# Gate projection of two token groups by seven block products, and output sums formed in PSUM banks

## The chip, the cores and the metric

The kernel runs on one core of a Trainium2 chip. Its time is the device time of one execution in microseconds (us). Five engines work side by side, each through its own list of instructions: TensorE (PE in the profile; PEld is its loading of weights), VectorE (DVE), ScalarE (ACT), GpSimd (POOL) and SyncE (SP). They wait for one another by semaphores. TensorE writes its products into PSUM, [...]; VectorE and ScalarE read them there.

## The reference

Attention with cosine-weighted features is followed by a gated feed-forward block.

```python
# q, k, v: (8, 8, 576, 64);  w_gate, w_val: (512, 1536);  w_out: (1536, 512)
q_p, k_p = phi(q, cos_w, sin_w), phi(k, cos_w, sin_w)      # relu, times cos and sin
kv = np.einsum('bhsf,bhsd->bhfd', k_p, v)
z = np.sum(k_p, axis=2)
num = np.einsum('bhsf,bhfd->bhsd', q_p, kv)
den = np.einsum('bhsf,bhf->bhs', q_p, z)[..., None] + 1e-06
attn_out = num / den
x = attn_out.transpose(0, 2, 1, 3).reshape(4608, 512)
g = x @ w_gate
silu = g * (1.0 / (1.0 + np.exp(-g)))
val = x @ w_val
return silu * val @ w_out                                  # (4608, 512), float32
```

## The kernel before

The 4608 tokens are worked through in nine groups (`tg` 0 to 8) of 512. A group has a projection part of 12 blocks `fc` of 128 features, and then an output stage. Beside them, in numbered slots, runs the attention work of later groups: `phi_q` (the `r_q` products), `vmul` and `kv_mm` per batch, and four attention tiles per group, whose result `x` is turned by DMA into `xT`, the input of the next group.

A block of the projections is eight matmuls of 512 columns, a silu on ScalarE and a multiplication on VectorE:

```python
def ffn_mm(tg, fc, ...):                    # cut to the case of a whole group
    st["f", ...] = [take(1)[:, 0:n] for _ in range(2)]       # two PSUM banks
    for i in which:                                          # gate, then value
        for kc in range(KC):
            nc.tensor.matmul(out=st["f", ...][i], lhsT=(wg_sb, wv_sb)[i][:, kc, fs], rhs=xT[tg][:, ts, kc], ...)
def ffn_silu(...):  nc.scalar.activation(out=sg, in_=gate, func=AF.Silu, scale=DOWN)
def ffn_mul(...):   nc.vector.tensor_tensor(out=ht[:, fc], in0=sg, in1=value, op=ALU.mult)
```

An attention tile takes two neighbouring banks, and VectorE makes `den`, `rec` and `x` out of them:

```python
def a_tile2(t):
    ps = take(2)
    ...                                     # 8 or 16 small matmuls into ps
    x_of(t, ps)                             # den, rec, x on VectorE
```

The output stage of groups 2 to 8 multiplies 512 tokens x 1536 features by 1536 x 512 weights, as seven block products in place of eight (the form of Strassen's scheme by Winograd). `aq` are the quarters of `ht`, `bq` those of the weights; `S1` to `S4` are sums of the token side, made on VectorE (`token_sum`), `T1` to `T4` sums of the weights, made once. A product is 12 matmuls of 256 columns.

```python
a = home("a")
product(a, aq[:, 0, 0], bq[:, 0, 0], True)
nc.scalar.mul(out=C12, in_=a[0], mul=DOWN)
e = home("e")
product(e, S3, T3, True)
added(C22, e, C12)                          # VectorE: C22 = e * DOWN + C12
b = home("b", nb)
product(b, S2, T2, True)
added(C21, b, C22)
token_sum(4, 4, 6)
slot_of(0)
product(a, aq[:, 1, 0], bq[:, 1, 0], False)
nc.scalar.mul(out=C11, in_=a[0], mul=DOWN)
slot_of(1)
product(b, S1, T1, False)
added(C22, b, C22)
c = home("c")
product(c, aq[:, 1, 1], T4, True)
added(C21, c, C21)
slot_of(2)                                  # (stores are left out here)
product(b, S4, bq[:, 1, 1], False)
added(C12, b, C12)
slot_of(3)
```

Banks are given out by `take`, which picks the free bank that was used longest ago.

Of the kernel before, what the change touches and what calls it, by code (L numbers as in the profile page):

```python
# [10 lines left out]
FP32 = mybir.dt.float32  # L11
# [7 lines left out]
def kernel(  # L19
# [29 lines left out]
    HT = T // 2  # L49
    HD = d_model // 2  # L50

    consts = ctx.enter_context(tc.tile_pool(name="consts", bufs=1))
    raw = ctx.enter_context(tc.tile_pool(name="raw", bufs=3))
    rel = ctx.enter_context(tc.tile_pool(name="rel", bufs=1))
# [3 lines left out]
    smp = ctx.enter_context(tc.tile_pool(name="smp", bufs=3))  # L58
    sgp = ctx.enter_context(tc.tile_pool(name="sgp", bufs=5))
    obp = ctx.enter_context(tc.tile_pool(name="obp", bufs=2))  # L60
    psum = ctx.enter_context(tc.tile_pool(name="psum", bufs=1, space=bass.MemoryType.PSUM))
# [8 lines left out]

    def take(n, hold=None):

        taken = {x for r in held.values() for x in r}
        free = [b for b in range(0, 8, n) if not any(b <= x < b + n for x in taken)]

        b0 = min(free, key=lambda b: (n == 1 and hold is not None and hold[0] == "o" and b ^ 1 not in taken,
                                      sorted(used[b:b + n], reverse=True)))
        if hold is not None:
            held[hold] = range(b0, b0 + n)
        touch(range(b0, b0 + n))  # L80
        return banks[:, b0] if n == 1 else banks[:, b0:b0 + n]
# [16 lines left out]
    def raw_of(b, nm):  # L98
        if (b, nm) not in raws:
            raws[b, nm] = raw.tile([P, G, NC, D], BF16, name=f"raw_{nm}")  # L100
        return raws[b, nm]
# [51 lines left out]
    make_identity(nc, ident)  # L153
    kvd = []
    for j in range(2):
        t = consts.tile([P, 8 * J * D1], BF16, name=f"kvd_{j}")
        if j:
            nc.gpsimd.memset(t.bitcast(FP32), 0.0)
        kvd.append(t.rearrange("p (e j w i x) -> p e j w i x", e=2, j=J, w=2, i=2))


# [43 lines left out]
    )  # L205
    v2s = []
    for j in range(2):
        t = consts.tile([P, G, NC, 2, W], BF16, name=f"v2_{j}")
        nc.vector.tensor_copy(out=t[:, :, :, :, D], in_=csk.unsqueeze(1).to_broadcast([P, G, NC, 2]))
        v2s.append(t)  # L210


    wg_sb = consts.tile([P, KC, d_ff], BF16)
    wv_sb = consts.tile([P, KC, d_ff], BF16)
    wg_r = moe_w_gate.rearrange("(c p) f -> p c f", p=P)
# [38 lines left out]
    def vmul(b, g):  # L254
        nc.vector.tensor_tensor(  # L255
            out=v2s[b % 2][:, g, :, :, 0:D],
            in0=(first if b == 0 and g == 0 else {"v": raw_of(b, "v")})["v"][:, g].unsqueeze(2).to_broadcast([P, NC, 2, D]),
            in1=tab, op=ALU.mult,
        )
# [34 lines left out]
    def kv_mm(b):  # L294
        ps = st[b, "kvps"] = take(2, ("kv", b))
        for j, c in [(j, c) for j in range(J) for c in range(NC)]:
            for i in range(2):
                for e in range(2):
                    es = slice(e * SH, (e + 1) * SH)
                    g = 2 * j + i  # L300
                    nc.tensor.matmul(  # L301
                        out=ps[i * D:(i + 1) * D, e, j * 2 * D1:(j + 1) * 2 * D1],
                        lhsT=raws[b, "k"][es, g, c],
                        rhs=v2s[b % 2][es, g, c, :, 0:D1],
                        start=(c == 0), stop=(c == NC - 1),
                    )
# [50 lines left out]

    qf = consts.tile([P, 2, J, 2, D], BF16)
    qr = [lodge(4 * J * SH, BF16).rearrange("p (e j c s) -> p e j c s", e=2, j=J, c=2) for i in range(2)]
# [70 lines left out]
    def x_rec(t, ps, ys=slice(0, 4)):  # L430
        if ys.start == 0:
            st["rec", t] = smp.tile([P, H, 1], FP32, name="rec")
            st["x", t] = xp.tile([P, d_model], BF16, name="x")
        nc.vector.reciprocal(out=st["rec", t].rearrange("p (e y) o -> p e y o", e=2)[:, :, ys],
                             in_=st["den", t].rearrange("p (e y) o -> p e y o", e=2)[:, :, ys])
# [41 lines left out]
    def x_norm(t):  # L477
        num = st.pop(("num", t)).rearrange("p j e (i x) -> p (j e i) x", i=2)
        den = smp.tile([P, H, 1], FP32, name="den")
        nc.vector.tensor_scalar(out=den, in0=num[:, :, D:D1], scalar1=1e-6, scalar2=DOWN,  # L480
                                op0=ALU.add, op1=ALU.mult)
        rec = smp.tile([P, H, 1], FP32, name="rec")
        nc.vector.reciprocal(out=rec, in_=den)
        x = xp.tile([P, d_model], BF16, name="x")
        for j in range(J):
            hs = slice(4 * j, 4 * j + 4)
            nc.vector.tensor_tensor(
                out=x[:, 4 * j * D:(4 * j + 4) * D].rearrange("p (i e d) -> p e i d", i=2, e=2),
                in0=num[:, hs, 0:D].rearrange("p (e i) d -> p e i d", e=2),
                in1=rec[:, hs].rearrange("p (e i) o -> p e i o", e=2).to_broadcast([P, 2, 2, D]), op=ALU.mult,  # L490
            )
        st["x", t] = x

    def xT_of(t):
        tg, off = divmod(t, GH // 2)
        if tg not in xT:
            xT[tg] = xtp.tile([P, GH // 2, KC, P], BF16, name="xT")
        return xT[tg][:, off]

    def x_turn_pe(t, ks=slice(0, KC)):  # L500
        ps = take(1, ("xt", t, ks.start)).bitcast(BF16).rearrange("p (k x) -> p k x", x=P)
        for kc in range(ks.start, ks.stop):
            nc.tensor.transpose(out=ps[:, kc], in_=st["x", t][:, kc * P:(kc + 1) * P], identity=ident)  # L503
        st["xt", t, ks.start] = ps[:, ks]
# [13 lines left out]
    def ffn_mm(tg, fc, lo=0, hi=GH, which=(0, 1)):  # L518
# [4 lines left out]
        if 0 in which:  # L523
# [3 lines left out]
            else:  # L527
                st["f", tg, fc, lo] = [take(1)[:, 0:n] for _ in range(2)]
        for i in which:
# [21 lines left out]
    def ffn_fc(*a):  # L551

        ffn_mm(*a)
        ffn_act(*a)

    out_v = out.rearrange("(b p c) f -> b c p f", p=SH, c=NC)
# [24 lines left out]
    def ffn_out(t, f0=0, f1=None):  # L581

        f1 = FC if f1 is None else f1
        if f0 == 0:
            o_ps[t] = take(1, ("o", t))
        r = t % OUT * P
# [39 lines left out]
    def out_by_quarters(tg, slot_of):  # L626
# [7 lines left out]

        def home(nm, parts=1):
            return [take(1, ("o", tg, nm, i)).rearrange("p (t x) -> p t x", x=HD) for i in range(parts)]

# [3 lines left out]

        def at_of(x, i):
            return x[i][:, 0] if len(x) == 2 else x[0][:, i]

        def product(to, a, b, first):
            for i in range(2):
                for kc in range(HC):
                    nc.tensor.matmul(out=at_of(to, i), lhsT=a[:, kc, i * P:(i + 1) * P], rhs=b[:, kc],  # L648
                                     start=first and kc == 0 and (i == 0 or len(to) == 2),
                                     stop=kc == HC - 1, skip_group_check=True)  # L650

        def added(o, ps, x):
            for i in range(len(ps)):
                sl = slice(i, i + 1) if len(ps) == 2 else slice(0, 2)
                nc.vector.scalar_tensor_tensor(out=o[:, sl], in0=ps[i][:, 0:1] if len(ps) == 2 else ps[i],  # L655
                                               scalar=DOWN, in1=x[:, sl], op0=ALU.mult, op1=ALU.add)

        nb = 2 if last else 1
        a = home("a")
        product(a, aq[:, 0, 0], bq[:, 0, 0], True)  # L660
        nc.scalar.mul(out=C12, in_=a[0], mul=DOWN)
        e = home("e")
        product(e, S3, T3, True)
        added(C22, e, C12)
        b = home("b", nb)
        free("e")
        product(b, S2, T2, True)
        added(C21, b, C22)
        token_sum(4, 4, 6)
        slot_of(0)  # L670
        product(a, aq[:, 1, 0], bq[:, 1, 0], False)
        nc.scalar.mul(out=C11, in_=a[0], mul=DOWN)
        free("a")
# [3 lines left out]
        product(b, S1, T1, False)  # L677
        added(C22, b, C22)
        if last:
            store_two(t0 + 2, slice(HD, d_model))  # L680
        c = home("c")
        product(c, aq[:, 1, 1], T4, True)
        added(C21, c, C21)
        free("c")
# [6 lines left out]
        product(b, S4, bq[:, 1, 1], False)  # L691
        added(C12, b, C12)
        free("b", nb)
# [171 lines left out]
    for b in range(2, B):  # L865
# [17 lines left out]
        at(tk[-1], lambda b=b: kv_mm(b), lambda b=b: kv_out2(b))  # L883
        at(tk[-1] + 1, lambda b=b: kv_free(b))
    for t in range(2 * OUT, NTG * OUT):
        tg, i = divmod(t, OUT)
# [12 lines left out]
    for tg in range(1, NTG):  # L899
        s0 = SLOTS * tg  # L900
        for fc in range(FC):
            ffn_fc(tg, fc)
# [41 lines left out]
```

## Time and profile before

| | |
|---|---|
| time | 318.63 us, median of 3 runs (318.44 to 318.73) |
| span of the profiled execution | 316.5 us |
| busy on TensorE, VectorE, ScalarE | 308.6, 225.0, 130.1 us |
| span of group 7, projections and output stage (251.00 to 281.92) | 30.9 us: TensorE 30.9 busy, VectorE 19.2, ScalarE 8.4 |
| span of group 8's projections (281.92 to 302.64) | 20.7 us |

A row of the profile's groups names the line of the kernel, the engine, the operation, what it writes and reads, the shape and the count; then busy time and the mean of one in ns; then how long the engine was idle ahead of it, and what ended that. The chain that ended last is followed back from the last instruction. The timeline gives start, length, engine, line and operation, and in brackets the idle time ahead and its releaser.

### The profile page before, as it was taken

The page shows a single profiled execution, that of the slowest core. Times are in us where ns is not written, and L with a number is a line of the kernel's source. Part 1 is how long each engine was busy: PE and PEld are TensorE (multiplying, and loading weights), DVE is VectorE, ACT ScalarE, POOL GpSimd, SP SyncE. Part 2 cuts the span into 40 slices and gives each one's busy share as a digit, 9 for nine tenths or more (in the row PEclk, how much of TensorE's full clock was granted, in tenths as well). Part 3 has the DMA queues.
Part 4 walks back from the last instruction along what each step waited for, and adds up shares of the span by engine and source line. Part 5 has one row for each costly group of instructions (what it writes and reads, how often), then busy time and mean ns, then how long its engine had stood idle before and what let it go on. Part 6 is the DMA issues. An engine that isn't in the chain of part 4 may idle for free.

```text
span 316.5 us, 6619 instructions
## 1 busy us (share of the span) xinstructions
PE 308.6 (98%) x2624; PEld 182.7 (58%) x2624; DVE 225.0 (71%) x448; ACT 130.1 (41%) x237; POOL 35.7 (11%) x60
## 2 busy tenths in 40 slices
PE   8899999999999999999999999999999999999994
PEld 4597455455445485548554855477456745774473
DVE  7873777797658898598858875888578437843662
ACT  7554545753435354334533343334432133213320
POOL 6754202000200200030003000300000000000000
PEclk9999999999999999999999999999999999999999
DMA  7999999998896985989497989598951241233004
GB/s 256 223 198 197 206 205 136 226 130 110 143 220 90 174 117 133 134 107 199 111 141 86 194 158 139 69 195 135 156 78 35 59 92 24 39 68 71 2 0 133
DMA packets 74766, 41.06 MB, mean 130 GB/s; under 512 B 49904, under 2 KB 69872, under 8 KB 74736
## 3 DMA queue, kind: packets, MB, share of 16 engines
q1 hardware_dynamic: 51952, 22.55, 40.1%
q0 software_dynamic: 22192, 17.57, 37.3%
q10 hardware_dynamic: 592, 0.52, 0.5%
q8 instruction: 20, 0.33, 0.4%
q14 instruction: 10, 0.08, 0.1%
HBM read 37.75 MB, written 9.44 MB: 149 GB/s over the span
## 4 chain that ended last, share of the span: by engine, by line
PE 92%; DMA 2%; DVE 2%; ACT 2%; issue 0%; ACTq 0%
PE banks L531 59%; PE banks L648 18%; PE banks L588 6%; PE banks L301 3%; PE banks L415 2%; DMA xT<-x 2%; PE banks L461 1%; PE banks L397 1%; DVE v L255 1%; PE banks L168 1%; PE banks L341 0%; PE banks L503 0%; ACT L200 0%; ACT phit L349 0%; ACT kvd L313 0%
## 5 line engine op out<-in xcount | busy, mean ns | idle before, releaser
L537 ACT ACTIVATE sg<-banks 128x512 bf16<-128x512 f32 (+2 forms) x116 | 65.8, 568 | 118.8 <-PE banks L531 111.3
L531 PE MATMUL banks<-xT,wg_sb 128*128 128x512 bf16 (+2 forms) x464 | 111.3, 364 | 0.6 <-DMA xT<-x 0.6
L542 DVE TENSOR_TENSOR ht<-sg,banks 128x512 f16<-128x512 bf16 (+2 forms) x116 | 74.5, 648 | 52.3 <-PE banks L531 45.3
L531 PE MATMUL banks<-xT,wv_sb 128*128 128x512 bf16 (+2 forms) x464 | 111.3, 364 | 0.0
L531 PEld LDWEIGHTS <-wv_sb 128*128 128x128 bf16 x464 | 44.9, 98 | 48.7
L531 PEld LDWEIGHTS <-wg_sb 128*128 128x128 bf16 x464 | 43.1, 98 | 42.3 <-issue 0.8
L655 DVE SCALAR_TENSOR_TENSOR ob<-banks,ob 128x512 f32<-128x512 f32 (+1 forms) x38 | 24.6, 648 | 14.4 <-PE banks L648 13.4
L648 PEld LDWEIGHTS <-ht 128*128 128x128 f16 x336 | 32.4, 98 | 3.9
L648 PEld LDWEIGHTS <-sums 128*128 128x128 f16 x252 | 24.6, 98 | 3.6 <-issue 0.8
L255 DVE TENSOR_TENSOR v<-raw_v,tab 128x1152 bf16<-128x1152 bf16 x31 | 22.7, 751 | 0.2 <-ACT raw_v L701 0.2
L588 PE MATMUL banks<-wo_sb,ht 128*128 128x512 f16 x96 | 22.7, 379 | 0.0
L438 DVE TENSOR_TENSOR x<-banks,rec 128x512 bf16<-128x512 f32 (+1 forms) x32 | 21.6, 674 | 1.3 <-PE banks L397 0.3
L648 PE MATMUL banks<-wo_sb,ht 128*128 128x256 f16 x168 | 20.6, 273 | 0.0
L648 PE MATMUL banks<-wt_sb,sums 128*128 128x256 f16 x168 | 19.5, 273 | 0.0
L648 PE MATMUL banks<-wt_sb,ht 128*128 128x256 f16 x168 | 19.5, 273 | 0.0
L251 DVE TENSOR_TENSOR r_q<-raw_q,tab 128x1152 bf16<-128x1152 bf16 x24 | 17.6, 752 | 2.7 <-ACT raw_q L234 2.4
L234 ACT ACTIVATE raw_k<-raw_k 128x576 bf16<-128x576 bf16 (+1 forms) x25 | 17.0, 694 | 0.0
L850 POOL COPY hold<-phit 1x2 bf16<-1x2 bf16 x5 | 1.2, 244 | 130.6 <-DMA phit<-r_q 130.6
L619 DVE TENSOR_TENSOR sums<-ht 128x1024 f16<-128x1024 f16 (+1 forms) x28 | 15.5, 552 | 0.2
L234 ACT ACTIVATE raw_q<-raw_q 128x576 bf16<-128x576 bf16 x24 | 14.9, 674 | 0.0
L588 PEld LDWEIGHTS <-ht 128*128 128x128 f16 x96 | 9.1, 98 | 8.9 <-issue 0.2
L415 PEld LDWEIGHTS <-phit 128*128 128x128 bf16 (+1 forms) x240 | 10.0, 100 | 6.5 <-issue 1.3
(95 smaller groups left out, 209.8 us busy)
## 6 DMA issues: line engine op xcount, KB each, us to landing
out_dram<-ob SPq DMA_DIRECT2D x67, 128.0 KB, 2.4
raw_k<-in_k_dram POOLq DMA_DIRECT2D x7, 576.0 KB, 9.3
raw_q<-in_q_dram POOLq DMA_DIRECT2D x6, 576.0 KB, 6.7
raw_v<-in_v_dram POOLq DMA_DIRECT2D x6, 576.0 KB, 11.7
wo_sb<-in_moe_w_out_dram POOLq DMA_DIRECT2D x3, 512.0 KB, 12.8
wg_sb<-in_moe_w_gate_dram POOLq DMA_DIRECT2D x5, 256.0 KB, 9.1
wv_sb<-in_moe_w_val_dram POOLq DMA_DIRECT2D x5, 256.0 KB, 9.4
wo_sb<-in_v_dram SPq DMA_DIRECT2D x2, 576.0 KB, 4.2
```

Of the source, the lines that this page charges most:

```text
L234: nc.scalar.activation(out=out, in_=in_, func=AF.Relu)
L251: nc.vector.tensor_tensor(out=st[b, "q"][:, g], in0=o.unsqueeze(2).to_broadcast([P, NC, 2, D]), in1=tab, op=ALU.mult)
L255: nc.vector.tensor_tensor(out=v2s[b % 2][:, g, :, :, 0:D], in0=(first if b == 0 and g == 0 else {"v": raw_of(b, "v")})["v"][:, g].unsqueez ...
L415: nc.tensor.matmul(out=ps[ms, e, g * D1:(g + 1) * D1], lhsT=phit[b][:, e, g, c:c + n].rearrange("p c s -> p (c s)"), rhs=kv2s[b % 2][:, e, ...
L438: nc.vector.tensor_tensor(out=st["x", t].rearrange("p (y e d) -> p e y d", e=2, d=D)[:, :, ys], in0=ps[:, :, 0:2 * J * D1].rearrange("p e ...
L531: nc.tensor.matmul(out=st["f", tg, fc, lo][i], lhsT=(wg_sb, wv_sb)[i][:, kc, fs], rhs=xT[tg][:, ts, kc], start=(kc == 0), stop=(kc == KC - 1))
L537: nc.scalar.activation(out=sg[:, 0:n], in_=st["f", tg, fc, lo][0], func=AF.Silu, scale=DOWN)
L542: nc.vector.tensor_tensor(out=ht[:, fc, r:r + n], in0=st.pop(("s", tg, fc, lo))[:, 0:n], in1=ps[1], op=ALU.mult)
L588: nc.tensor.matmul(out=o_ps[t], lhsT=ht[:, fc, r:r + P], rhs=wo_sb[:, fc], start=(fc == 0), stop=(fc == FC - 1))
L619: nc.vector.tensor_tensor(out=o[:, lo:hi], in0=x[:, lo:hi], in1=y[:, lo:hi], op=op)
L648: nc.tensor.matmul(out=at_of(to, i), lhsT=a[:, kc, i * P:(i + 1) * P], rhs=b[:, kc], start=first and kc == 0 and (i == 0 or len(to) == 2), ...
L655: nc.vector.scalar_tensor_tensor(out=o[:, sl], in0=ps[i][:, 0:1] if len(ps) == 2 else ps[i], scalar=DOWN, in1=x[:, sl], op0=ALU.mult, op1= ...
```

## The change

It does two things.

The gate projection of groups 7 and 8 (`GATE`) takes seven block products for eight as well. The gate's weights are seen as two by two blocks (`A11` to `A22`: the two halves of the 512 inputs, and the even and odd blocks of features), and so is the group's `xT` (`B11` to `B22`: input halves and token halves). `W1` to `W4` are sums of weight blocks, made once on VectorE in the output stage of group 5; `X1` to `X4` are sums of blocks of x, made in the output stage ahead of each of the two groups. A gated group runs in three thirds `u`, each with seven products of four matmuls of 256 columns and four value projections `V`, which stay as they were. Sums of products are formed in PSUM: ScalarE copies a finished product into another bank, on which the next product adds [...], and VectorE adds the copy `m7` to a bank. x and both projections' weights are held in fp16 for bfloat16.

In the output stage of groups 2 to 8 the sums are formed in PSUM in the same manner, so that of five additions on VectorE two stay, with a copy, and ScalarE gets two more copies.

To make room, `k` and `v` have two load buffers in place of three, and the sums' buffers lie over buffers of the first groups.

```diff
+    GATE = (7, 8)
-    raw = ctx.enter_context(tc.tile_pool(name="raw", bufs=3))
+    raw = ctx.enter_context(tc.tile_pool(name="raw", bufs=2))
+    rawq = ctx.enter_context(tc.tile_pool(name="rawq", bufs=3))
...
-    def take(n, hold=None):
+    def take(n, hold=None, fills=False, seeded=False):
-        free = [b for b in range(0, 8, n) if not any(b <= x < b + n for x in taken)]
+        free = [b for b in range(0, 8, n) if not any(b <= x < b + n for x in taken)
+                and (filled[b] or not seeded)]
...
-    wg_sb = consts.tile([P, KC, d_ff], BF16)
-    wv_sb = consts.tile([P, KC, d_ff], BF16)
+    wg_sb = consts.tile([P, KC, d_ff], FP16)
+    wv_sb = consts.tile([P, KC, d_ff], FP16)
...
+    def gate_weight_sum(n):
+        o, x, y, op = ((W1, A21, A22, ALU.add), (W2, W1, A11, ALU.subtract), (W3, A11, A21, ALU.subtract),
+                       (W4, A12, W2, ALU.subtract))[n]
+        nc.vector.tensor_tensor(out=o, in0=x, in1=y, op=op)
...
+        for u in range(3):
+            a = bank("a", fills=True)
+            product(a, u, A11, B11, True)
+            b = bank("b", seeded=True)
+            nc.scalar.copy(out=b, in_=a)
+            e = bank("e", fills=True)
+            product(e, u, W3, X3, True)
+            m7 = m7p.tile([P, 2, HT], FP32, name="m7")
+            nc.scalar.copy(out=m7, in_=e)
+            free("e")
+            V(*((u - 1, 1, 1) if u else (u, 0, 0)))
+            done()
+            product(b, u, W2, X2, False)
+            c = bank("c", seeded=True)
+            nc.vector.tensor_tensor(out=c, in0=m7, in1=b, op=ALU.add)
+            product(a, u, A12, B21, False)
+            silu(u, 1, 0, a)
+            free("a")
+            if u:
+                mul(u - 1, 1, 1)
+            if u == 2:
+                for n in (1, 2):
+                    token_sum(n, 0, 4)
+            V(u, 0, 0) if u else V(u, 1, 0)
+            done()
+            product(b, u, W1, X1, False)
+            nc.vector.tensor_tensor(out=m7, in0=m7, in1=b, op=ALU.add)
+            silu(u, 0, 1, m7)
+            product(c, u, A22, X4, False)
+            silu(u, 0, 0, c)
+            free("c")
+            V(u, 1, 0) if u else V(u, 0, 1)
+            mul(u, 0, 0)
+            mul(u, 1, 0)
+            if u:
+                token_sum(3, *((0, 4) if u == 1 else (4, 6)))
+            done()
+            product(b, u, W4, B22, False)
+            silu(u, 1, 1, b)
+            free("b")
+            if u:
+                V(u, 0, 1)
+            mul(u, 0, 1)
+            if u:
+                done()
+            if u == 2:
+                token_sum(4, 0, 4)
+        V(2, 1, 1)
+        mul(2, 1, 1)
+        for n in (1, 2):
+            token_sum(n, 4, 6)
+        done()
...
-        nc.scalar.mul(out=C12, in_=a[0], mul=DOWN)
-        e = home("e")
+        b = home("b", nb, seeded=True)
+        for p_, o_ in each(b, a[0]):
+            nc.scalar.copy(out=p_, in_=o_)
+        e = home("e", fills=True)
         product(e, S3, T3, True)
-        added(C22, e, C12)
-        b = home("b", nb)
+        nc.scalar.mul(out=C22, in_=e[0], mul=DOWN)
+        c = home("c", seeded=True)
         free("e")
-        product(b, S2, T2, True)
-        added(C21, b, C22)
+        product(b, S2, T2, False)
+        for p_, o_, x_ in each(b, c[0], C22):
+            nc.vector.scalar_tensor_tensor(out=o_, in0=x_, scalar=UP, in1=p_, op0=ALU.mult, op1=ALU.add)
...
         product(b, S1, T1, False)
-        added(C22, b, C22)
+        for p_, x_ in each(b, C22):
+            nc.vector.scalar_tensor_tensor(out=x_, in0=p_, scalar=DOWN, in1=x_, op0=ALU.mult, op1=ALU.add)
-        c = home("c")
-        product(c, aq[:, 1, 1], T4, True)
-        added(C21, c, C21)
+        product(c, aq[:, 1, 1], T4, False)
+        copied("act", C21, c)
...
         product(b, S4, bq[:, 1, 1], False)
-        added(C12, b, C12)
+        copied("dve", C12, b)
...
+    for n in range(4):
+        at(SLOTS * (GATE[0] - 2) + FC + n, lambda n=n: gate_weight_sum(n))
+    for tg in GATE:
+        for n in range(4):
+            at(SLOTS * (tg - 1) + FC + (2, 2, 3, 3)[n], lambda tg=tg, n=(2, 0, 1, 3)[n]: x_sum(tg, n))
```

A call of `done()` runs the next slot; the attention tiles of the group ahead stand in slots 5, 7, 9 and 11 of a group.

More of the change, by code (lines that the diff above doesn't have):

```diff
@@ L50 @@
     HD = d_model // 2
+    KH = KC // 2
+    GATE = (7, 8)
     consts = ctx.enter_context(tc.tile_pool(name="consts", bufs=1))
-    raw = ctx.enter_context(tc.tile_pool(name="raw", bufs=3))
+    raw = ctx.enter_context(tc.tile_pool(name="raw", bufs=2))
+    rawq = ctx.enter_context(tc.tile_pool(name="rawq", bufs=3))
     rel = ctx.enter_context(tc.tile_pool(name="rel", bufs=1))
@@ L59 @@
     sgp = ctx.enter_context(tc.tile_pool(name="sgp", bufs=5))
+    sg2p = ctx.enter_context(tc.tile_pool(name="sg2p", bufs=3))
+    m7p = ctx.enter_context(tc.tile_pool(name="m7p", bufs=2))
     obp = ctx.enter_context(tc.tile_pool(name="obp", bufs=2))
@@ L69 @@
     held = {}
-    def take(n, hold=None):
+    filled = [False] * 8
+    def take(n, hold=None, fills=False, seeded=False):
         taken = {x for r in held.values() for x in r}
-        free = [b for b in range(0, 8, n) if not any(b <= x < b + n for x in taken)]
+        free = [b for b in range(0, 8, n) if not any(b <= x < b + n for x in taken)
+                and (filled[b] or not seeded)]
         b0 = min(free, key=lambda b: (n == 1 and hold is not None and hold[0] == "o" and b ^ 1 not in taken,
@@ L79, in take @@
             held[hold] = range(b0, b0 + n)
+        filled[b0:b0 + n] = [fills or seeded] * n
         touch(range(b0, b0 + n))
@@ L99, in raw_of @@
         if (b, nm) not in raws:
-            raws[b, nm] = raw.tile([P, G, NC, D], BF16, name=f"raw_{nm}")
+            raws[b, nm] = (rawq if nm == "q" else raw).tile([P, G, NC, D], BF16, name=f"raw_{nm}")
         return raws[b, nm]
@@ L154 @@
     kvd = []
+    kvt = consts.tile([P, 2, 8 * J * D1], BF16, name="kvt")
     for j in range(2):
-        t = consts.tile([P, 8 * J * D1], BF16, name=f"kvd_{j}")
+        t = kvt[:, j]
         if j:
@@ L159 @@
         kvd.append(t.rearrange("p (e j w i x) -> p e j w i x", e=2, j=J, w=2, i=2))
+    xs_sb = kvt.rearrange("p a b -> p (a b)")[:, 0:2 * KC * T // 2].bitcast(FP16).rearrange(
+        "p (n t c x) -> p n t c x", n=4, t=2, c=KH)
+    ident16 = consts.tile([P, P], FP16)
+    make_identity(nc, ident16)
     zeros = consts.tile([P, P], BF16)
@@ L206 @@
     v2s = []
+    wgs_sb = consts.tile([P, 4, KH, HC, P], FP16, name="wgs_sb")
     for j in range(2):
-        t = consts.tile([P, G, NC, 2, W], BF16, name=f"v2_{j}")
+        t = (wgs_sb.rearrange("p n c u x -> p (n c u x)")[:, 0:G * NC * 2 * W].bitcast(BF16).rearrange(
+            "p (g c e w) -> p g c e w", g=G, c=NC, e=2) if j else
+            consts.tile([P, G, NC, 2, W], BF16, name=f"v2_{j}"))
         nc.vector.tensor_copy(out=t[:, :, :, :, D], in_=csk.unsqueeze(1).to_broadcast([P, G, NC, 2]))
         v2s.append(t)
-    wg_sb = consts.tile([P, KC, d_ff], BF16)
-    wv_sb = consts.tile([P, KC, d_ff], BF16)
+    wg_sb = consts.tile([P, KC, d_ff], FP16)
+    wv_sb = consts.tile([P, KC, d_ff], FP16)
     wg_r = moe_w_gate.rearrange("(c p) f -> p c f", p=P)
@@ L255, in vmul @@
         nc.vector.tensor_tensor(
-            out=v2s[b % 2][:, g, :, :, 0:D],
+            out=v2s[b == 1][:, g, :, :, 0:D],
             in0=(first if b == 0 and g == 0 else {"v": raw_of(b, "v")})["v"][:, g].unsqueeze(2).to_broadcast([P, NC, 2, D]),
@@ L303, in kv_mm @@
                         lhsT=raws[b, "k"][es, g, c],
-                        rhs=v2s[b % 2][es, g, c, :, 0:D1],
+                        rhs=v2s[b == 1][es, g, c, :, 0:D1],
                         start=(c == 0), stop=(c == NC - 1),
@@ L355, in kv_first_out @@
             give_back(("kvf", j))
-    qf = consts.tile([P, 2, J, 2, D], BF16)
+    qf = wgs_sb.rearrange("p n c u x -> p (n c u x)")[:, G * NC * 2 * W:G * NC * 2 * W + 4 * J * D].bitcast(
+        BF16).rearrange("p (c j i d) -> p c j i d", c=2, j=J, i=2)
     qr = [lodge(4 * J * SH, BF16).rearrange("p (e j c s) -> p e j c s", e=2, j=J, c=2) for i in range(2)]
@@ L432, in x_rec @@
             st["rec", t] = smp.tile([P, H, 1], FP32, name="rec")
-            st["x", t] = xp.tile([P, d_model], BF16, name="x")
+            st["x", t] = xp.tile([P, d_model], FP16, name="x")
         nc.vector.reciprocal(out=st["rec", t].rearrange("p (e y) o -> p e y o", e=2)[:, :, ys],
@@ L483, in x_norm @@
         nc.vector.reciprocal(out=rec, in_=den)
-        x = xp.tile([P, d_model], BF16, name="x")
+        x = xp.tile([P, d_model], FP16, name="x")
         for j in range(J):
@@ L496, in xT_of @@
         if tg not in xT:
-            xT[tg] = xtp.tile([P, GH // 2, KC, P], BF16, name="xT")
+            xT[tg] = xtp.tile([P, GH // 2, KC, P], FP16, name="xT")
         return xT[tg][:, off]
     def x_turn_pe(t, ks=slice(0, KC)):
-        ps = take(1, ("xt", t, ks.start)).bitcast(BF16).rearrange("p (k x) -> p k x", x=P)
+        ps = take(1, ("xt", t, ks.start)).bitcast(FP16).rearrange("p (k x) -> p k x", x=P)
         for kc in range(ks.start, ks.stop):
-            nc.tensor.transpose(out=ps[:, kc], in_=st["x", t][:, kc * P:(kc + 1) * P], identity=ident)
+            nc.tensor.transpose(out=ps[:, kc], in_=st["x", t][:, kc * P:(kc + 1) * P], identity=ident16)
         st["xt", t, ks.start] = ps[:, ks]
@@ L527, in ffn_mm @@
             else:
-                st["f", tg, fc, lo] = [take(1)[:, 0:n] for _ in range(2)]
+                st["f", tg, fc, lo] = [take(1, fills=n == 512)[:, 0:n] for _ in range(2)]
         for i in which:
@@ L554, in ffn_fc @@
         ffn_act(*a)
+    wg4 = wg_sb.rearrange("p (k c) (u w x) -> p w k c u x", k=2, w=2, x=P)
+    A11, A12, A21, A22 = wg4[:, 1, 0], wg4[:, 1, 1], wg4[:, 0, 0], wg4[:, 0, 1]
+    W1, W2, W3, W4 = (wgs_sb[:, i] for i in range(4))
+    X1, X2, X3, X4 = (xs_sb[:, i] for i in range(4))
+    def gate_weight_sum(n):
+        o, x, y, op = ((W1, A21, A22, ALU.add), (W2, W1, A11, ALU.subtract), (W3, A11, A21, ALU.subtract),
+                       (W4, A12, W2, ALU.subtract))[n]
+        nc.vector.tensor_tensor(out=o, in0=x, in1=y, op=op)
@@ new lines, in x_parts, with x_sum, ffn_by_quarters, bank @@
+    def x_parts(tg):
+        return (xT[tg][:, 2 * j:2 * j + 2, KH * k:KH * k + KH] for k in range(2) for j in range(2))
+    def x_sum(tg, n):
+        B11, B12, B21, B22 = x_parts(tg)
+        o, x, y = ((X1, B12, B11), (X2, B22, X1), (X3, B22, B12), (X4, B21, X2))[n]
+        nc.vector.tensor_tensor(out=o, in0=x, in1=y, op=ALU.subtract)
+    def ffn_by_quarters(tg, slot_of):
+        B11, B12, B21, B22 = x_parts(tg)
+        val, gates, count = {}, {}, [0]
+        def bank(nm, **kw):
+            return take(1, ("g", tg, nm), **kw).rearrange("p (i x) -> p i x", i=2)
+        def free(nm):
+            give_back(("g", tg, nm))
+        def product(to, u, a, x, first):
+            for i in range(2):
+                for c in range(KH):
+                    nc.tensor.matmul(out=to[:, i], lhsT=a[:, c, 2 * u + i], rhs=x[:, :, c],
+                                     start=first and i == 0 and c == 0, stop=c == KH - 1, skip_group_check=True)
+        def silu(u, w, j, src):
+            if (u, w) not in gates:
+                gates[u, w] = sg2p.tile([P, 2, T], BF16, name="sg2")
+            nc.scalar.activation(out=gates[u, w][:, :, j * HT:(j + 1) * HT], in_=src, func=AF.Silu, scale=DOWN)
+        def V(u, i, w):
+            fc = 4 * u + 2 * i + w
+            val[u, i, w] = take(1, ("v", tg, fc), fills=True)
+            for kc in range(KC):
+                nc.tensor.matmul(out=val[u, i, w], lhsT=wv_sb[:, kc, fc * P:(fc + 1) * P], rhs=xT[tg][:, :, kc],
+                                 start=(kc == 0), stop=(kc == KC - 1))
+        def mul(u, i, w):
+            fc = 4 * u + 2 * i + w
+            nc.vector.tensor_tensor(out=ht[:, fc], in0=gates[u, w][:, i], in1=val.pop((u, i, w)), op=ALU.mult)
+            give_back(("v", tg, fc))
+        def done():
+            slot_of(count[0])
+            count[0] += 1
+        for u in range(3):
[50 more added lines that the diff above has]
+        done()
@@ L584, in ffn_out @@
         if f0 == 0:
-            o_ps[t] = take(1, ("o", t))
+            o_ps[t] = take(1, ("o", t), fills=True)
         r = t % OUT * P
@@ L633, in out_by_quarters, with home @@
         C21, C22 = (obs[t0 // 2 + 1][:, :, x * HD:(x + 1) * HD] for x in range(2))
-        def home(nm, parts=1):
-            return [take(1, ("o", tg, nm, i)).rearrange("p (t x) -> p t x", x=HD) for i in range(parts)]
+        def home(nm, parts=1, **kw):
+            return [take(1, ("o", tg, nm, i), **kw).rearrange("p (t x) -> p t x", x=HD) for i in range(parts)]
         def free(nm, parts=1):
@@ L640, in free @@
                 give_back(("o", tg, nm, i))
-        def at_of(x, i):
-            return x[i][:, 0] if len(x) == 2 else x[0][:, i]
         def product(to, a, b, first):
@@ L647, in product, with each, copied @@
                 for kc in range(HC):
-                    nc.tensor.matmul(out=at_of(to, i), lhsT=a[:, kc, i * P:(i + 1) * P], rhs=b[:, kc],
-                                     start=first and kc == 0 and (i == 0 or len(to) == 2),
+                    nc.tensor.matmul(out=to[i][:, 0] if len(to) == 2 else to[0][:, i],
+                                     lhsT=a[:, kc, i * P:(i + 1) * P], rhs=b[:, kc],
+                                     start=first and kc == 0 and i == 0,
                                      stop=kc == HC - 1, skip_group_check=True)
[L652 to L656, printed above, removed]
+        def each(ps, *others):
+            if len(ps) == 1:
+                return [(ps[0], *others)]
+            return [(ps[i][:, 0:1], *(o[:, i:i + 1] for o in others)) for i in range(2)]
+        def copied(eng, o, ps, x=DOWN):
+            for p_, o_ in each(ps, o):
+                if eng == "act":
+                    nc.scalar.mul(out=o_, in_=p_, mul=x)
+                else:
+                    nc.vector.tensor_single_scalar(out=o_, in_=p_, scalar=x, op=ALU.mult)
         nb = 2 if last else 1
-        a = home("a")
+        a = home("a", fills=True)
         product(a, aq[:, 0, 0], bq[:, 0, 0], True)
-        nc.scalar.mul(out=C12, in_=a[0], mul=DOWN)
-        e = home("e")
+        b = home("b", nb, seeded=True)
+        for p_, o_ in each(b, a[0]):
+            nc.scalar.copy(out=p_, in_=o_)
+        e = home("e", fills=True)
         product(e, S3, T3, True)
-        added(C22, e, C12)
-        b = home("b", nb)
+        nc.scalar.mul(out=C22, in_=e[0], mul=DOWN)
+        c = home("c", seeded=True)
         free("e")
-        product(b, S2, T2, True)
-        added(C21, b, C22)
+        product(b, S2, T2, False)
+        for p_, o_, x_ in each(b, c[0], C22):
+            nc.vector.scalar_tensor_tensor(out=o_, in0=x_, scalar=UP, in1=p_, op0=ALU.mult, op1=ALU.add)
         token_sum(4, 4, 6)
@@ L671, in out_by_quarters @@
         product(a, aq[:, 1, 0], bq[:, 1, 0], False)
-        nc.scalar.mul(out=C11, in_=a[0], mul=DOWN)
+        copied("act", C11, a)
         free("a")
@@ L900 @@
         s0 = SLOTS * tg
-        for fc in range(FC):
+        if tg in GATE:
+            ffn_by_quarters(tg, lambda i: slot(s0 + i))
+        for fc in range(FC) if tg not in GATE else ():
             ffn_fc(tg, fc)
```

## The prediction

> **What bounds the kernel now.** I read the page's table of engines first, then the chain that ended last, then the stretches of the last groups in the order of time.
>
> ```profile
> PE 308.6 (98%) x2624; PEld 182.7 (58%) x2624; DVE 225.0 (71%) x448; ACT 130.1 (41%) x237; POOL 35.7 (11%) x60
> ...
> PE 92%; DMA 2%; DVE 2%; ACT 2%; issue 0%; ACTq 0%
> ```
>
> TensorE is busy 98% of the span and is 92% of the chain: a matmul taken out shortens the kernel, if nothing else then makes TensorE wait. The chain in order of time (start, length, what) gives the price of each kind of product:
>
> ```profile
> 209.21 7.86 PE banks L648 x72
> 217.06 0.03 issue
> ...
> 251.00 10.36 PE banks L531 x48
> ...
> 272.75 9.17 PE banks L648 x84
> 281.92 20.72 PE banks L531 x96
> 302.64 9.18 PE banks L648 x84
> 311.84 0.42 DVE ob L655
> ```
>
> Group 8's gate and value projections are 96 matmuls of 512 columns in 20.72 us, 216 ns each; an output stage is 84 matmuls of 256 columns in 9.18 us, 109 ns each. They run back to back. The 0.03 at 217.06 matters: there TensorE just barely waits for something in group 5's output stage. The timeline of that stage (start, length, engine, line) shows for what:
>
> ```profile
> 213.17 0.69 DVE L655 SCALAR_TENSOR_TENSOR ob<-banks,ob 128x512 f32<-128x512 f32 x1 [0.56 <-PE banks L648]
> 213.78 0.41 DVE L619 TENSOR_TENSOR sums<-ht,sums 128x512 f16<-128x512 f16 x1
> 214.11 1.42 DVE L251 TENSOR_TENSOR r_q<-raw_q,tab 128x1152 bf16<-128x1152 bf16 x2
> 214.28 2.78 PE L648 MATMUL banks<-wt_sb,ht 128*128 128x256 f16 x24
> ...
> 215.68 0.76 DVE L251 TENSOR_TENSOR r_q<-raw_q,tab 128x1152 bf16<-128x1152 bf16 x1
> ...
> 216.36 1.44 DVE L655 SCALAR_TENSOR_TENSOR ob<-banks,ob 128x512 f32<-128x512 f32 x2
> 217.09 1.47 PE L648 MATMUL banks<-wo_sb,sums 128*128 128x256 f16 x12
> ```
>
> VectorE works through three r_q products before it reaches the addition that reads bank b (216.36, the C22 one). The seventh product, which writes b again, starts at 217.09, 0.04 after that addition's first part ends at 217.05. So in this stage VectorE has no slack at all ahead of the seventh product. Prices on VectorE and ScalarE, from the costliest groups with forms kept apart (busy, mean ns):
>
> ```profile
> L542 DVE TENSOR_TENSOR ht<-sg,banks 128x512 f16<-128x512 bf16 x102 | 69.7, 685 | 47.6 <-PE banks L531 45.3 <-PE banks L461 1.2 <-PE banks L290 0.5
> L537 ACT ACTIVATE sg<-banks 128x512 bf16<-128x512 f32 x102 | 60.9, 597 | 113.9 <-PE banks L531 107.1 <-ACT raw_k L234 5.0 <-DVE sums L619 1.6
> L610 DVE TENSOR_TENSOR wt_sb<-wo_sb 128x1536 f16<-128x1536 f16 x2 | 1.9, 949 | 0.0
> L619 DVE TENSOR_TENSOR sums<-ht 128x1024 f16<-128x1024 f16 x14 | 9.6, 683 | 0.0
> ```
>
> An independent VectorE operation starts some 0.07 before the one ahead of it shows its end (235.66, 0.69 long, then 236.27), so I count a row of them at 0.61 for 512 columns out of PSUM, 0.60 for a 1024 sum, 0.33 for a 512 sum, and the full length plus 0.04 where one reads the other's result. A tile of x (den, rec, x) is 0.2 + 0.23 + 0.61. From a matmul's last slot to its reader the timeline shows 0.2, from a reader's end to TensorE 0.04.
>
> [...] its fp16 matmuls (L588, L648) keep the same pace as bf16 ones. [...] the C22 addition's input was complete at 215.6, and it ran at 216.36, after the r_q products. [...] (685 ns for 512 from PSUM, 949 for 1536 fp16), so I put an addition m7 + b at 0.69.
>
> **The change, part by part.**
>
> Matmuls. Per gated group the gate loses 48 x 215.9 ns = 10.36 us and gets 3 x 28 x 109.3 = 9.18: 1.18 saved, 2.36 for two groups. The value projection and the output stage keep their matmuls. fp16 changes no duration.
>
> Output stages (groups 2 to 8). Five VectorE additions become two and a copy; ScalarE gets two more (bank b's seed, and C21). TensorE waited 0.03 per stage, so there is nothing to win. The seed must be there before the third product: its source ends 1.31 after the start, plus 0.2 and 0.6 makes 2.1, and the third product starts at 2.62. No wait.
>
> Weight sums: four of 0.95 each, on VectorE in group 5's output stage. When the kernel is built, VectorE's instructions there stand as: c, token sum, r_q, r_q, W1, r_q, W2, C22 addition, r_q, W3, copy of C12, v, W4. So W1 and W2 come ahead of the addition that has no slack. At a pace of 0.88 each they push it by 1.76, less the 0.15 that VectorE idled before the third r_q: the seventh product starts 1.6 later. W3 and W4 fall behind it, where group 6's eight banks let TensorE run on. Cost **+1.6**.
>
> Group 7's gate, in us from its first matmul (a block product of four matmuls is 0.44, a value projection 0.86, an attention tile 0.26). The first third runs freely: 5.65. But a multiplication into `ht` now waits for a silu that comes last in its third (m7, add, silu, silu), so VectorE idles early and is crowded late. In the second third the silu of c ends at 11.65, and then VectorE has in this order two multiplications, a token sum, an x tile, a multiplication: it gets through at 15.3. TensorE, at 14.17, wants the next attention tile into the same two banks, which the x tile frees at 14.75: wait 0.6. Then x tile, c (to 17.04; the product W1 X1 was due 16.79: wait 0.3), a multiplication, two token sums, m7 (to 19.7; W4 B22 was due at 19.08: wait 0.65). The silus of m7 and c end at 20.9, two multiplications, a half sum and x tile follow to 23.73; the last attention tile was due at 21.9: wait 1.85. So the output stage starts at 24.0, against 21.76 before (20.72 and four tiles of 0.26). Sum of the waits 3.4, less 1.18: **+2.2**.
>
> Group 8's gate has no attention tiles. Same reckoning: one wait of 0.55 for m7 in the last third; the output stage starts at 20.1; its third product waits 0.5 for the last part of S2, which comes behind the late multiplications. The group ends at 29.8, against 29.90: **-0.1**.
>
> Sums of x (four of 512 per group) come in output stages that have VectorE room: 0. The tail after the last matmul is a copy in place of an addition of the same 0.42: 0.
>
> Sum: 1.6 + 2.2 - 0.1 = +3.7. 318.63 + 3.7 = **322.3 us**.
>
> **Rivals.** (1) The saving arrives whole: 318.63 - 2.36 = 316.3. For it: TensorE is 98% of the span, VectorE has 19.2 of 30.9 us busy in group 7 before. Against it: the order above; a mean share says nothing of a queue that is crowded for the last third. (2) Only one of the two queues bites, since my paces are pessimistic or the weight sums cost alone: between 318.0 and 320.5. (3) The engine-written accumulators cost more than counted: were ScalarE's seed late by 0.5 in each of seven stages, or the PSUM-to-PSUM operations slower than 0.6 and 0.69, it would be 324 to 326. Against it: 0.5 us of margin at the seed, and ScalarE is at 41%. (4) Fewer buffers for k and v (two for three) delay loads: each load's buffer was last read a group earlier, so I give it nothing.
>
> **Range and chances.** The waits in group 5 and group 7 are worked out from measured durations and a fixed order, so I hold the centre near their sum; 0.3 us of error in each of the six waits gives about 2 either way, and rival (1) in part stretches the low side: 317.4 to 324.6. 2% is 6.4 us (312.3 and 325.0): faster 0.01, within 0.94, slower 0.05.
>
> **What would show it.** Group 5's output stage: a wait of 1.6 ahead of the seventh product, the C22 addition behind W2. Group 7: TensorE idle ahead of the attention tiles and of products into b, its output stage some 24.0 after the gate's start; group 8's at 20.1. Groups 2 to 4 unchanged to 0.1. I am wrong if TensorE stays back to back in groups 5 and 7, if the seeds show up as waits, or if groups 2 to 4 change.

## The result, and the profile after

The changed kernel takes 321.35 us (median of 4 runs, 321.21 to 321.55), the kernel before 318.53 on the same chip: ratio 1.0091, 95% interval 1.0074 to 1.0109. It is slower by 0.9%, 2.8 us; the prediction was 3.7 slower.

The page's table of engines and its shares of the chain that ended last, of the changed kernel:

```profile
PE 307.6 (96%) x2696; PEld 189.8 (59%) x2696; DVE 229.0 (72%) x458; ACT 143.6 (45%) x264; POOL 35.7 (11%) x62
...
PE 86%; DVE 9%; ACT 3%; issue 1%; DVEq 0%; ACTq 0%
```

TensorE's busy time is only 1.0 us lower (308.6 before), and VectorE is now 9% of the chain where it was 2%. The span grew from 316.5 to 319.5, and TensorE's busy share fell: the time went into TensorE waiting. The stages, measured from the start of one to the start of the next in the two timelines (up to 175.93 the two agree within 0.01, so groups 2 and 3 are unchanged, and group 5's projections take 23.03 in both):

| stage | before | after | difference | predicted |
|---|---|---|---|---|
| output stage of group 4, with the wait for xT ahead of group 5 | 10.08 | 9.63 | -0.45 | 0 |
| output stage of group 5 | 9.36 | 10.92 | +1.56 | +1.6 |
| group 6 | 32.43 | 32.43 | 0 | 0 |
| group 7 | 30.92 | 33.06 | +2.14 | +2.2 |
| group 8, up to its last VectorE operation | 30.09 | 30.02 | -0.07 | -0.1 |
| from there to the end of the span | 4.66 | 4.48 | -0.18 | 0 |

The chain that ended last (start, length, what) in group 5's output stage of the changed kernel:

```profile
208.75 3.94 PE banks L772 x36
212.99 0.41 issue
213.40 0.42 DVE sums L746
213.81 1.34 DVE r_q L268 x2
215.15 0.87 DVE wgs_sb L582
216.12 0.49 issue
216.61 0.95 DVE wgs_sb L582
217.56 0.61 DVE ob L813
218.21 1.47 PE banks L772 x12
```

Before, this stage was one run of TensorE. Now the chain leaves TensorE after the third product and goes through VectorE: two r_q products, the first weight sum (0.87), a third r_q product that the chain shows as "issue", the second weight sum (0.95), the C22 addition (L813), and only then the seventh product. The timeline gives its wait as 1.59; from when it was due (213.83 plus 24 matmuls of 0.109, 216.45) to its start it is 1.76, against 0.19 in the kernel before (due 216.90, start 217.09).

In the last third of group 7's gate, the timeline of the changed kernel (idle time and releaser in brackets at the end of a row):

```profile
265.23 1.03 PE L618 MATMUL banks<-xT,wv_sb 128*128 128x512 f16 x4
...
266.73 0.42 PE L433 MATMUL banks<-kv,phit 128*128 128x65 bf16 x8 [0.48 <-DVE x L456]
...
267.86 1.03 PE L618 MATMUL banks<-xT,wv_sb 128*128 128x512 f16 x4
...
268.24 0.69 DVE L644 TENSOR_TENSOR banks<-m,banks 128x512 f32<-128x512 f32 x1
...
268.83 0.68 DVE L623 TENSOR_TENSOR ht<-sg,banks 128x512 f16<-128x512 bf16 x1
268.97 0.60 PE L606 MATMUL banks<-kvt,wgs_sb 128*128 128x256 f16 x4
...
269.54 0.69 DVE L746 TENSOR_TENSOR ht<-ht 128x1024 f16<-128x1024 f16 x1
...
270.27 0.69 DVE L746 TENSOR_TENSOR sums<-ht 128x1024 f16<-128x1024 f16 x1
...
270.71 0.42 PE L433 MATMUL banks<-kv,phit 128*128 128x65 bf16 x8
270.88 0.68 DVE L656 TENSOR_TENSOR m<-m,banks 128x512 f32<-128x512 f32 x1
...
271.61 0.60 PE L606 MATMUL banks<-xT,wgs_sb 128*128 128x256 f16 x4 [0.48 <-DVE m L656]
...
272.05 1.89 PE L618 MATMUL banks<-xT,wv_sb 128*128 128x512 f16 x8
...
274.83 0.69 DVE L456 TENSOR_TENSOR x<-banks,rec 128x512 f16<-128x512 f32 x1
...
275.57 0.42 PE L433 MATMUL banks<-kv,phit 128*128 128x65 bf16 x8 [1.64 <-DVE x L456]
...
275.83 1.47 PE L772 MATMUL banks<-wo_sb,ht 128*128 128x256 f16 x12
```

VectorE is back to back from c (L644) to m7 (L656) with a multiplication and two token sums between them, and TensorE's product W4 B22 at 271.61 waits for m7. The largest wait is that of the last attention tile, at 275.57, for the x tile before it. The gate started at 251.94, so the output stage starts 23.89 after it.

### The profile page after: what moved, and what is told of

Same layout as the page of the kernel before. It is cut to its first block, busy times and chain, and to the rows that moved or that the text cites. A ratio compares the mean times of both kernels' runs of the same rounds, so it can differ in the third digit from the quotient of the medians.

```text
span 319.5 us, 6775 instructions
## 1 busy us (share of the span) xinstructions
PE 307.6 (96%) x2696; PEld 189.8 (59%) x2696; DVE 229.0 (72%) x458; ACT 143.6 (45%) x264; POOL 35.7 (11%) x62
## 4 chain that ended last, share of the span: by engine, by line
PE 86%; DVE 9%; ACT 3%; issue 1%; DVEq 0%; ACTq 0%
PE banks L549 46%; PE banks L772 18%; PE banks L715 6%; PE banks L606 4%; PE banks L618 4%; PE banks L318 3%; PE banks L433 2%; DVE ht L623 2%; DVE sums L746 1%; ACT sg L612 1%; PE banks L479 1%; PE banks L415 1%; DVE v L272 1%; DVE m L656 1%; DVE ht L746 1%
## 5 line engine op out<-in xcount | busy, mean ns | idle before, releaser
L549 PE MATMUL banks<-xT,wg_sb 128*128 128x512 f16 (+2 forms) x368 | 86.6, 360 | 0.1
L549 PE MATMUL banks<-xT,wv_sb 128*128 128x512 f16 (+2 forms) x368 | 86.6, 360 | 0.0
L555 ACT ACTIVATE sg<-banks 128x512 bf16<-128x512 f32 (+2 forms) x92 | 51.5, 560 | 77.7 <-PE banks L549 75.1
L560 DVE TENSOR_TENSOR ht<-sg,banks 128x512 f16<-128x512 bf16 (+2 forms) x92 | 58.0, 638 | 32.4 <-PE banks L549 25.7
L549 PEld LDWEIGHTS <-wv_sb 128*128 128x128 f16 x368 | 35.4, 98 | 37.4
L549 PEld LDWEIGHTS <-wg_sb 128*128 128x128 f16 x368 | 33.8, 98 | 31.7 <-issue 0.4
L772 PEld LDWEIGHTS <-ht 128*128 128x128 f16 x336 | 32.5, 98 | 3.9
L618 PE MATMUL banks<-xT,wv_sb 128*128 128x512 f16 x96 | 24.3, 379 | 0.0
L456 DVE TENSOR_TENSOR x<-banks,rec 128x512 f16<-128x512 f32 (+1 forms) x32 | 21.6, 674 | 1.5 <-PE banks L415 0.3
L623 DVE TENSOR_TENSOR ht<-sg,banks 128x512 f16<-128x512 bf16 x24 | 15.7, 682 | 7.3 <-ACT sg L612 7.3
```

The source lines that it names most:

```text
L456: nc.vector.tensor_tensor(out=st["x", t].rearrange("p (y e d) -> p e y d", e=2, d=D)[:, :, ys], in0=ps[:, :, 0:2 * J * D1].rearrange("p e ...
L549: nc.tensor.matmul(out=st["f", tg, fc, lo][i], lhsT=(wg_sb, wv_sb)[i][:, kc, fs], rhs=xT[tg][:, ts, kc], start=(kc == 0), stop=(kc == KC - 1))
L555: nc.scalar.activation(out=sg[:, 0:n], in_=st["f", tg, fc, lo][0], func=AF.Silu, scale=DOWN)
L560: nc.vector.tensor_tensor(out=ht[:, fc, r:r + n], in0=st.pop(("s", tg, fc, lo))[:, 0:n], in1=ps[1], op=ALU.mult)
L618: nc.tensor.matmul(out=val[u, i, w], lhsT=wv_sb[:, kc, fc * P:(fc + 1) * P], rhs=xT[tg][:, :, kc], start=(kc == 0), stop=(kc == KC - 1))
L623: nc.vector.tensor_tensor(out=ht[:, fc], in0=gates[u, w][:, i], in1=val.pop((u, i, w)), op=ALU.mult)
```

## The experiments

All times are medians on the same chip as the kernel before, which read 318.33 in the first four and 318.48 in the last four.

### The weight sums elsewhere

```diff
-        at(SLOTS * (GATE[0] - 2) + FC + n, lambda n=n: gate_weight_sum(n))
+        at(SLOTS * (GATE[0] - 1) + (3, 4, 6, 8)[n], lambda n=n: gate_weight_sum(n))
```

> The changed kernel with its four weight sums moved from group 5's output stage to slots 3, 4, 6 and 8 of group 6's projections. If they cost because they stand ahead of the C22 addition in VectorE's queue: group 5's output stage goes from 10.9 back to 9.4 us, group 6 stays at 32.4, and the time is 1.5 us under the changed kernel's 321.35, so 319.8. If they cost wherever they stand (3.8 us of VectorE work): still about 321.3, and group 6 gets longer.

319.69 us, ratio 1.0044 (1.0031 to 1.0058). Group 5's output stage is 9.35 again, group 6 stays at 32.43 with the four sums in it. The chain of this kernel at that place is TensorE alone again:

```profile
209.38 7.86 PE banks L772 x72
217.27 1.47 PE banks L772 x12
```

The same four operations cost 1.6 in one place and nothing in another.

### The output sums alone

```diff
-    GATE = (7, 8)
+    GATE = ()
-    for n in range(4):
+    for n in range(0):                       # no weight sums
```

> The changed kernel without gated groups: no gate products, no weight sums, no sums of x; the output stages with sums formed in PSUM, the buffers and fp16 stay. If the seeds and the PSUM-to-PSUM additions hide: the time of the kernel before within 0.5 us, 318.1 to 318.7, each output stage at 9.3. If each of seven stages waits for ScalarE's seed by 0.4 or more: over 321.

317.81 us, ratio 0.9984 (0.9975 to 0.9992): 0.5 less, 0.3 under the lower edge of the first expectation, and far from the second. The seeds and the sums in PSUM are not what makes the change slow. That holds for fp16 and for the two load buffers of k and v as well, which this version has too; only their sum with the output sums is measured. Part of the half microsecond is at the end: from the start of the last VectorE operation to the end of the span it takes 4.46 against 4.66 in the kernel before. What else it holds was not separated.

### The attention tiles elsewhere

```diff
+            if tg == 8:
+                s = SLOTS * 6 + FC + i
             at(s, lambda t=t: a_tile2(t), turn(t))
```

> The changed kernel with the four attention tiles of the last group moved out of group 7's gate into group 6's output stage (slots 12 to 15). If group 7 is long because those tiles stand in a crowded VectorE queue: its length (projections and output stage) goes from 33.1 to 29.9, like group 8's, group 6 grows by the tiles' own 1.04, and the time falls by about 2.2 to 319.2. If the seven products wait for their own additions and silus rather than for the tiles: under 0.8 less, so above 320.5.

319.09 us, ratio 1.0021 (1.0011 to 1.0031). Group 7 is 29.81 long (252.71 to 282.52). The tiles' 1.04 now lie in group 6; the rest, 2.2, is gone. They are the same tiles with the same VectorE work; only their place has changed.

### Both moves

The two edits together.

> Both moves: weight sums in group 6's projections, attention tiles in group 6's output stage. If the two costs are apart and add up: 1.5 + 2.2 under 321.35, so 317.6, a little under the kernel before. If one hides behind the other, or group 6 gets too full for VectorE: 318.5 or more.

317.69 us, ratio 0.998 (0.9973 to 0.9987). The two costs are apart and add up. But 317.7 is no more than what the output sums alone give: a gated group without any attention work takes 29.9, just what it took with eight products. Who waited for whom in the two gated groups of this kernel, TensorE alone (total us, times, longest):

```profile
engine line waited for: us in total, times, longest us
PE banks L606 <- DVE m L656: 0.9, 2, 0.5
PE banks L772 <- DVE sums L746: 0.8, 2, 0.4
```

Per group, one wait for m7 and one for a token sum: what the seven products save goes there.

### The sums in another order

```diff
             if u:
                 mul(u - 1, 1, 1)
-            if u == 2:
-                for n in (1, 2):
-                    token_sum(n, 0, 4)
             ...
             nc.vector.tensor_tensor(out=m7, in0=m7, in1=b, op=ALU.add)
+            if u == 2:
+                for n in (1, 2):
+                    token_sum(n, 0, 4)
             ...
-            if u == 2:
-                token_sum(4, 0, 4)
         V(2, 1, 1)
         mul(2, 1, 1)
         for n in (1, 2):
             token_sum(n, 4, 6)
+        token_sum(4, 0, 4)
```

> Both moves of the last kernel, and in the last third of a gated group the token sums S1 and S2 (blocks 0 to 3) put behind the addition to m7, and S4 (blocks 0 to 3) behind the last parts of S1 and S2. Both-moves still shows TensorE waiting 0.47 for m7 and 0.4 for a token sum in each gated group. If these waits are again only the order in VectorE's queue, they go, and the whole saving of the seven products (2.36) is there: 317.69 - 1.7 = 316.0. If the last third simply has more VectorE work than TensorE work, the waits turn up elsewhere: 317.3 or more.

315.36 us, ratio 0.9907 (0.9891 to 0.9923): faster than both kernels. The end of its chain:

```profile
270.37 1.73 PE banks L618 x8
272.09 9.17 PE banks L771 x84
...
299.07 1.73 PE banks L618 x8
300.79 9.18 PE banks L771 x84
310.00 0.42 DVE ob L786
```

From the end of a gate into the output stage TensorE goes without a step between. Group 7 is 28.7 long (252.40 to 281.10), 1.2 less than its 29.9 with eight products (tiles not counted): the whole saving. The two thirds of S1 and S2 (blocks 0 to 3 of 6) that stood ahead of m7 now run in the time that VectorE spends waiting for the silus in the both-moves version (1.24 there ahead of the next multiplication, at 270.70). Which of the two moves, that of S1 and S2 or that of S4, gives how much was not separated. The step from both moves to this is 2.3, not the 1.7 that I expected; why is told in the last section.

### Two sums in the kernel before, ahead and behind

The kernel before, with nothing of the change, and two extra sums of 1536 columns into a buffer that nobody reads, so nothing is left out of its result.

```diff
+    scratch = consts.tile([P, HC, HD], FP16, name="scratch")
+    def extra_sum(n):
+        nc.vector.tensor_tensor(out=scratch, in0=(bq[:, 0, 1], bq[:, 1, 1])[n],
+                                in1=(bq[:, 0, 0], bq[:, 1, 0])[n], op=ALU.subtract)
+    for n in range(2):
+        at(SLOTS * 5 + FC + (0, 1)[n], lambda n=n: extra_sum(n))     # behind: (2, 3)[n]
```

> The kernel before, with two extra sums of 1536 columns on VectorE (into a scratch buffer that nobody reads) in slots 12 and 13 of group 5: ahead of the C22 addition in group 5's output stage. No gate, no seed, no fp16. If the place in the queue is the cost, this alone makes 318.3 into 319.9: the wait ahead of the seventh product goes from 0.03 to 1.6.

> The kernel before with the same two extra sums in slots 14 and 15 of group 5: behind the C22 addition. If the place in the queue is the cost: 318.3 as without them, no wait ahead of the seventh product beyond 0.03. If VectorE's work as such costs in this stage: 319 or more.

Ahead: 319.97 us, ratio 1.0047 (1.0029 to 1.0065). Behind: 318.43, ratio 1.0005 (0.9995 to 1.0015). The timelines of the two, first ahead:

```profile
214.71 0.95 DVE L615 TENSOR_TENSOR scratch<-wo_sb 128x1536 f16<-128x1536 f16 x1
...
216.24 0.95 DVE L615 TENSOR_TENSOR scratch<-wo_sb 128x1536 f16<-128x1536 f16 x1
217.11 1.28 DVE L661 SCALAR_TENSOR_TENSOR ob<-banks,ob 128x512 f32<-128x512 f32 x2
217.85 1.47 PE L654 MATMUL banks<-wo_sb,sums 128*128 128x256 f16 x12 [1.53 <-DVE ob L661]
```

and behind:

```profile
217.06 1.44 DVE L661 SCALAR_TENSOR_TENSOR ob<-banks,ob 128x512 f32<-128x512 f32 x2
...
217.80 1.47 PE L654 MATMUL banks<-wo_sb,sums 128*128 128x256 f16 x12
...
219.08 0.95 DVE L615 TENSOR_TENSOR scratch<-wo_sb 128x1536 f16<-128x1536 f16 x1
```

Two operations on data that nobody needs reproduce the loss of group 5, by their place in the queue alone.

### Three gated groups

The fastest version (the sums in another order, the first of these four in the expectation below), with `GATE = (6, 7, 8)`.

> As the first of these four, with group 6 gated too (weight sums in group 5's projections). Group 6 has four attention tiles, the v products and the kv casts on VectorE beside its gate. If a gated group pays where attention work stands in the same queue: group 6 gets longer by 1 to 3 in place of shorter by 1.2, so 317 to 319. If the crowd in group 7 was a matter of those four slots alone: 1.2 less than the two-group version, 314.9.

318.66 us, ratio 1.0009 (0.9995 to 1.0023): 3.3 over the two-group version. The time lies in the first expectation; the group's own 3.3 is a little over the 1 to 3 expected. TensorE's waits in group 6's projections:

```profile
PE banks L606 <- DVE x L456: 1.2, 1, 1.2
PE banks L433 <- DVE x L456: 1.1, 1, 1.1
PE banks L606 <- DVE kvt L590: 0.9, 2, 0.5
PE banks L433 <- DVE ht L623: 0.2, 1, 0.2
```

Group 6's projections are 26.5 long, against 23.25 in the two-group version. Attention tiles are again most of what its products and tiles wait behind. The third row is the sums of x for group 6: VectorE reaches the first two (219.16) only behind an r_q product (218.48), when group 6's gate has begun (218.58), and the other two (221.10) behind a copy and a v product.

## Why the prediction was right

The place and the size of each term of the sum held; the waits below are counted from when TensorE was due (the start of the row ahead, plus 0.216 for each of its matmuls of 512 columns, 0.109 for 256, as in the reordered version's 1.73 for eight and 9.17 for 84, and 0.26 for a tile, as from 266.73 to 266.99 in the changed kernel) to when it started.

- **The saving.** 1.18 per group was put down for seven products. It is there (1.18 in group 7 and 1.19 in group 8), but only the reordered version shows it; in the changed kernel it is swallowed by waits. fp16 kept the pace of bf16: in the kernel before 48 matmuls of 512 columns take 10.36 in either (fp16 at 77.45, bf16 at 251.00).
- **Weight sums ahead of an addition without slack.** Predicted +1.6, measured 1.56. The two sums in the kernel before make it more than an argument: 1.5 ahead, 0 behind.
- **Group 7's queue.** The four waits were predicted as 0.6, 0.3, 0.65 and 1.85. Measured: 0.63 (tile due at 266.10, started 266.73), 0.25, 0.64 and 1.79 (due 273.78, started 275.57). The output stage starts 23.9 after the gate, predicted 24.0. The addition to m7, put at 0.69, took 0.68 (270.88). Moving the tiles takes the loss away.
- **Group 8.** Predicted waits 0.55 and 0.5; measured 0.62 for m7 and 0.49 for the token sum. Its output stage starts at 20.1, as predicted.
- **The seed hides.** In group 5's output stage of the changed kernel it runs from 210.15 to 210.72, and the product that needs it was due at 211.21. The version with output sums alone bears it out.
- **A wait that I misread.** I took the chain's 0.03 for the wait ahead of the seventh product in the kernel before and saw nothing to win in the output stages. From due to start it is 0.19, and the output stages of groups 2, 3 and 5 take 9.36 there, those of groups 6 and 7 9.18 and 9.17. The change leaves it as it is (9.35 and 9.36 in groups 2 and 3), so the sum did not suffer; putting the r_q products behind the addition was not tried.
- **What I had at zero and was not.** The prediction came out 0.9 too slow. 0.45 of it is the wait for xT ahead of group 5, from due to start 0.72 in the profile of before and 0.27 in that of after; 0.18 is the tail, which is shorter in all versions with the new output stage (4.40 to 4.48 in seven profiles) than in those with the old one (4.55 to 4.66 in three). The tail belongs to the change, and I had it at 0; its cause was not tried. The wait for xT does not: it is between 0 and 1.1 in the other versions' profiles, without a pattern that follows an edit, so I count it as scatter of one profile. Of the rest, 0.07 is in the other rows of the table, and 0.2 is that the medians differ by 2.8 where the two profiled spans differ by 3.0.

Of the rivals, the first (the saving arrives whole) describes not this kernel but the reordered one. The second (one of the two queues alone bites) falls with the two moves, each of which gave back its own share. The third (costlier seeds) falls with the output sums alone, and so does the fourth (fewer buffers for k and v): that version has the two buffers and is not slower than the kernel before.

## What to carry to other kernels

VectorE took its operations in the order of its queue here: in the kernel before, the C22 addition, its input complete at 215.6, ran at 216.36, behind the r_q products. What an operation costs then depends on what stands behind it (here two sums of 0.95 cost 0 or 1.5): before adding work to such a queue, find the operation in that stage which the bound engine waits for with no slack, and put the new work behind it. A step that makes several results come late together (here the silus at the end of each third) turned spare time early in the stage into a queue later (in group 7's gate VectorE idled 1.18 ahead of 257.93 and 1.24 ahead of 263.63, and TensorE's tile was 1.79 late at 275.57); a mean busy share of 62% over the stage said nothing of it. Work that others don't yet need (sums, tiles of the next group) belongs into the gaps that the new dependences open, or into a stage with room, and the gain of 2.4 us was only there once it lay there.

## What the runs showed of the hardware that I had not expected

The idle time in brackets understates a wait of TensorE. The tile at 266.73 shows 0.48 and started 0.63 late; m7's product shows 0.48 and was 0.64 late. The rows of PE run on past the point at which the next matmul could start (four matmuls of 256 columns show 0.60 and are followed after 0.44), and the idle time is counted from that end (265.23 plus 1.03 is 266.26, 0.47 ahead of 266.73). So the waits of the both-moves version, listed at 0.87 per group, were 1.2, and their removal brought 2.3 in place of 1.7. The same run-on is counted as busy (1.02 between 265.23 and 266.73, where four matmuls of 0.216 make 0.86): of the 2.36 of matmuls taken out, only 1.0 shows in TensorE's busy time, and six new waits (five in the two gates, one in group 8's output stage) at 0.16 each would make 1.0 of the missing 1.4, an estimate from these rows. Starts have to be compared with starts.
